# A third interleaved seven-product unit, and halves of keys and values folded by DMA, in a fused pooling-attention and SiLU kernel

## Chip, cores and metric

The kernel runs on one core of one Trainium2 chip. The metric is the device time of one execution in microseconds (us). Before the change three executions took 285.09, 285.44 and 285.60 us; the median is 285.44 us. The profile shown below is of one more execution, whose span is 284.4 us from the first to the last instruction.

## What is computed

```python
# q, k, v: (8 batches, 8 heads, 576 positions, 64), fp32
k_p = k.reshape(B, H, 72, 8, D).mean(axis=3)       # keys and values are averaged
v_p = v.reshape(B, H, 72, 8, D).mean(axis=3)       # over groups of 8 positions
attn = softmax(q @ k_p.T / sqrt(D))                # 576 x 72 for each head
x = (attn @ v_p)                                   # to (4608 tokens, 512)
h = x @ w_in                                       # 512 -> 2048
g = h * (1.0 / (1.0 + np.exp(-h)))                 # SiLU
out = g @ w_out                                    # 2048 -> 512, fp32
```

## The kernel before

The 4608 tokens are taken in nine tiles of 512 (`t` = 0 to 8). Each tile has an up-projection (`up`) with SiLU into `h_T` and then a down-projection (`down_quarters`). The attention of the batch `a = t + 1` is done in the gaps of the tile's instruction stream: a list of small functions ("fillers"), each with the number of the matmul step behind which it stands. So a filler's position fixes its place in the order of every engine's instructions; the engines themselves run each its own stream and wait for each other through semaphores.

The loads of one batch. A row of keys is 8 positions x 64 values in fp32. The first four positions are loaded plainly, and the other four are added onto them by a second load that accumulates. VectorE then adds the remaining four positions in two steps (4 to 2, and 2 to 1). All these loads are issued by GpSimd:

```python
def load_one(b, name):                       # first half: plain
    raw = raw_tile(f"{name}_raw", H)         # 72 x 8 x 256 fp32, one buffer for k, one for v
    nc.gpsimd.dma_start(out=raw, in_=source(b, name)[:, :, :PH])

def load_rest(b, name):                      # second half: added to the first by the DMA
    nc.gpsimd.dma_start(
        out=batches[b][f"{name}_raw"], in_=source(b, name)[:, :, PH:], accum_op=ALU.add)

def add_halves(raw):                         # 4 positions to 2, on VectorE (L183)
    nc.vector.tensor_add(
        out=raw[:, :, : 2 * D], in0=raw[:, :, : 2 * D], in1=raw[:, :, 2 * D :])

def add_rest(dst, raw):                      # 2 positions to 1, on VectorE (L188)
    nc.vector.tensor_add(out=dst, in0=raw[:, :, :D]..., in1=raw[:, :, D : 2 * D]...)

def pool_k(b, stage):
    if stage == 0: add_halves(raw); return
    for i in range(2): add_rest(kp[...], raw[...])

def pool_v(b):
    add_halves(st["v_raw"])
    add_rest(st["vp"]..., st["v_raw"])
```

The up-projection has 16 groups of 128 hidden columns. A plain group is four matmuls of 512 tokens, each over 128 of the 512 inputs. Four groups together can be done as one unit of the Strassen-Winograd kind: the block of 512 hidden columns by 512 tokens is split in quarters, and seven products of quarter size take the place of eight. Two units (groups 4 to 7 and 8 to 11) are done so in each tile from tile 1 on; the other eight groups are plain. A unit needs sums of quarters of the weights (made once), sums of quarters of x (`x_sum`, five per tile), and sums between its products:

```python
def stage(y, n):                                     # y: the unit, n: the step
    if n == "2":
        product(y, 2, "P", True);  nc.scalar.copy(r_sb, ps["P"])                # L499
    elif n == "5":
        product(y, 5, "Q", True);  tt(out=rr_sb, in0=ps["Q"], in1=r_sb, add)    # L502
    elif n == "1":
        product(y, 1, "R", True);  tt(out=t_sb, in0=ps["R"], in1=rr_sb, subtract)  # L505
    elif n == "4":
        product(y, 4, "P", False); hidden(y, 1, 0, ps["P"])     # SiLU on ScalarE, L490
    elif n == "3":
        product(y, 3, "Q", False); hidden(y, 0, 1, ps["Q"])
    elif n == "7":
        product(y, 7, "P", False); tt(out=c_sb[0], in0=ps["P"], in1=t_sb, add)  # L514
    elif n == "6":
        product(y, 6, "Q", False); tt(out=c_sb[1], in0=ps["Q"], in1=t_sb, add)  # L517
    elif n == "h": hidden(y, 0, 0, c_sb[0])
    else:          hidden(y, 1, 1, c_sb[1])                     # "s"
```

`product` issues four matmuls of 256 tokens (L482). P and Q stand in banks of the tag `at` (five banks, shared with the attention), R in one of the tag `mm` (three banks, shared with the plain groups, L541). `r_sb`, `rr_sb` and `t_sb` are one buffer each. The order of a tile from tile 2 on, and the fillers of loads and sums:

```python
items = (G(12, 13) + [(0, "251")] + G(14) + [(0, "43")] + G(15) + [(0, "76")]
    + [(1, "2")] + [(0, "hs")] + [(1, "51")] + G(0) + [(1, "43")] + G(1)
    + [(1, "7h6")] + G(2) + [(1, "s")] + G(3))
for n in U_X:                    # five sums of x at the head of the tile, L449
    f_up.append((0, lambda n=n: unit_x_sum(t, n)))
...
f_up.append((22, lambda: k_transpose(a)))
f_down.append((10, lambda: pool_v(a)))
...
for stage in range(2):           # the next batch's keys
    f_down.append((73 + 8 * stage, lambda stage=stage: pool_k(a + 1, stage)))
f_up.append((0, lambda: load_one(a + 1, "k")))
f_up.append((48 if a + 1 == B - 1 else 1, lambda: load_q(a + 1)))
f_up.append((2, lambda: load_rest(a + 1, "k")))
f_down.append((11, lambda: load_one(a + 1, "v")))
f_down.append((12, lambda: load_rest(a + 1, "v")))
```

The batches 3 to 7 are loaded in this way, in the tiles 1 to 5. Batches 0 to 2 are loaded and summed in another layout, which the change leaves alone.

Of the kernel before, what the change touches and what calls it, by code (L numbers as in the profile page):

```python
# [27 lines left out]
FP32 = mybir.dt.float32  # L28
FP32R = mybir.dt.float32r
BF16 = mybir.dt.bfloat16  # L30
# [6 lines left out]
def kernel(  # L37
# [73 lines left out]
    t_sb = singles.tile([128, 2, CQ], FP32, name="t_sb")  # L111
    xT = singles.tile([128, KF, NX], BF16, name="xT")

    w_sum1 = [singles.tile([128, 5, 2, 256], BF16, name=f"w_sum1{n}") for n in range(2)]
    x_sum = singles.tile([128, 5, 2, NQ], BF16, name="x_sum")
    c_sb = [singles.tile([128, 2, NQ], FP32, name=f"c_sb{n}") for n in range(2)]

# [61 lines left out]
            accum_op=ALU.add,  # L179
        )  # L180

    def add_halves(raw):
        nc.vector.tensor_add(  # L183
            out=raw[:, :, : 2 * D], in0=raw[:, :, : 2 * D], in1=raw[:, :, 2 * D :]
        )

    def add_rest(dst, raw):
# [3 lines left out]
            in1=raw[:, :, D : 2 * D].rearrange("k h (c d) -> k h c d", c=2),  # L191
        )

    def pool_k(b, stage):
        st = batches[b]
        raw = st["k_raw"]
        if stage == 0:
            add_halves(raw)
            return
        for i in range(2):  # L200
            add_rest(
                kp[:SP, i].rearrange("k c s d -> k s c d"), raw[:, 4 * i : 4 * (i + 1)]
            )

    def pool_v(b):
        st = batches[b]
        st["vp"] = mid.tile([SP, H, D], BF16, tag="vp", name="vp")
        add_halves(st["v_raw"])
        add_rest(st["vp"].rearrange("k h (c d) -> k h c d", c=2), st["v_raw"])

    def k_transpose(b, parts=(0, 1)):
# [207 lines left out]

    UNITS = ((4, 6), (8, 10))
    UW = [
        {
            (i, j): w_in_sb[:, 2 * j : 2 * j + 2, 128 * u : 128 * (u + 2)]
# [14 lines left out]
    def unit_weight_sum(y, n):  # L440
        a, b = U_W[n]
        nc.vector.tensor_tensor(
            out=w_sum1[y][:, U_WI[n]], in0=UW[y][a], in1=UW[y][b],
            op=ALU.subtract if n in (6, 7) else ALU.add,
        )

# [6 lines left out]

    def unit_weights(y, n):
        if n in U_WI:
            return w_sum1[y][:, U_WI[n]]
        return UW[y][0, 0] if n == 3 else UW[y][1, 1]

    def unit_x(t, n):
# [5 lines left out]
    def up(t, fillers, items):  # L465
        step = spread(
            fillers,
            sum(
                KF if len(it) == 3 else 2 * len(it[1].strip("hs")) for it in items
            ),  # L470
        )
        ps = {}

        def product(y, n, bank, first):
            if first:
                tag = "mm" if bank == "R" else "at"
                ps[bank] = ps_tile([128, 2, NQ], FP32, tag, f"u_ps{bank}")
            w, x = unit_weights(y, n), unit_x(t, n)
            for u in range(2):
                next(step)  # L480
                for kk in range(2):
                    nc.tensor.matmul(  # L482
                        ps[bank][:, u, :], lhsT=w[:, kk, 128 * u : 128 * (u + 1)],
                        rhs=x[:, kk, :], start=first and u == 0 and kk == 0,
                        stop=kk == 1, skip_group_check=True,
                    )

        def hidden(y, i, j, src):
            g = UNITS[y][i]
            nc.scalar.activation(  # L490
                h_T[:, g : g + 2, j * NQ : (j + 1) * NQ], src, func=AF.Silu
            )

        tt = nc.vector.tensor_tensor

        def stage(y, n):
            if n == "2":
                product(y, 2, "P", True)
                nc.scalar.copy(r_sb, ps["P"])  # L499
            elif n == "5":  # L500
                product(y, 5, "Q", True)
                tt(out=rr_sb, in0=ps["Q"], in1=r_sb, op=ALU.add)  # L502
            elif n == "1":
                product(y, 1, "R", True)
                tt(out=t_sb, in0=ps["R"], in1=rr_sb, op=ALU.subtract)  # L505
            elif n == "4":
                product(y, 4, "P", False)
                hidden(y, 1, 0, ps["P"])
            elif n == "3":
                product(y, 3, "Q", False)  # L510
                hidden(y, 0, 1, ps["Q"])
            elif n == "7":
                product(y, 7, "P", False)
                tt(out=c_sb[0], in0=ps["P"], in1=t_sb, op=ALU.add)  # L514
            elif n == "6":
                product(y, 6, "Q", False)
                tt(out=c_sb[1], in0=ps["Q"], in1=t_sb, op=ALU.add)  # L517
            elif n == "h":
                hidden(y, 0, 0, c_sb[0])
            else:  # L520
                hidden(y, 1, 1, c_sb[1])

        for it in items:
            if len(it) == 3:
                plain(t, step, *it)
            else:
                for n in it[1]:
                    stage(it[0], n)
        for _ in step:
            pass  # L530
# [248 lines left out]
    def load_half_2(name, half):  # L779
        for i0, i1 in ((0, SA), (SA, SLOTS), (SLOTS, SLOTS + 1)):  # L780
            load_slots(nc.gpsimd, 2, name, i0, i1, half)

    visits = [third(n) for n in range(3)]
    for t in range(NT):
        a = t + 1
        f_up, f_down = [], []
        if t == 0:
            GA = 11
            items = [(g, 0, HS) for g in range(GA)]
            items += [(g, HS, NTT - HS) for g in range(GA)]  # L790
            items += [(g, 0, NTT) for g in range(GA, KG)]
            f_up += [(1, lambda: denominators(0, part(0, 1), on_dve=True))]
            f_up += [(5, lambda: denominators(0, part(1, 1), on_dve=True))]
            f_up += [(13, lambda: numerators(0, part(0, 1)))]
            f_up += [(17, lambda: numerators(0, part(1, 1)))]
        else:
            G = lambda *gs: [(g, 0, NTT) for g in gs]
            if t == 1:
                items = (
                    G(12, 13, 14, 15) + [(0, "251")] + G(8) + [(0, "43")] + G(9)  # L800
                    + [(0, "7h6")] + G(10) + [(0, "s")] + G(11, 0, 1, 2, 3)
                )
            else:
                items = (
                    G(12, 13) + [(0, "251")] + G(14) + [(0, "43")] + G(15) + [(0, "76")]
                    + [(1, "2")] + [(0, "hs")] + [(1, "51")] + G(0) + [(1, "43")] + G(1)
                    + [(1, "7h6")] + G(2) + [(1, "s")] + G(3)
                )
            for n in U_X:
                f_up.append((0, lambda n=n: unit_x_sum(t, n)))  # L810
            for n in (2, 5):
                f_up.append((36 if t > 1 else 45, lambda n=n: hidden_sum(n, 4, 8)))
            f_up.append((56, lambda: hidden_sum(6, 4, 8)))
            for n, k0 in ((2, 0), (5, 0), (1, 4), (1, 0)):
                f_up.append((64, lambda n=n, k0=k0: hidden_sum(n, k0, k0 + 4)))
            f_down.append((33, lambda: hidden_sum(7, 0, 8)))
            f_down.append((71, lambda: hidden_sum(6, 0, 4)))
# [7 lines left out]
                if t == t0:  # L825
                    f_to.append((at + i, lambda n=n, i=i: weight_sum(n, i)))
        if a < B:
            q_at = [15, 16, 17, 8] if t > 1 else [24, 25, 26, 2] if t else [82, 84, 86, 88]
            if t == 0:
                for j in range(2):  # L830
                    f_up.append((44 + 8 * j, lambda j=j: slot_sums("k", j)))
# [5 lines left out]
            elif t == 1:  # L837
                for j in range(2):
                    f_up.append((0, lambda j=j: slot_sums("k", j, halves=True)))
                    f_up.append((22, lambda j=j: select_k(2, j)))  # L840
                    f_up.append((23, lambda j=j: copy_k(2, j)))
                    f_down.append((8, lambda j=j: slot_sums("v", j, halves=True)))
                    f_down.append((40, lambda j=j: select_v(2, j, "at")))
                    f_down.append((41, lambda j=j: copy_v(2, j)))
            else:
                f_up.append((22, lambda: k_transpose(a)))
                f_down.append((10, lambda: pool_v(a)))
            for n in range(4):
                f_to = f_down if t and n == 3 else f_up
                f_to.append((q_at[n], lambda n=n: q_transpose(a, n % 2, n // 2)))  # L850
            if t == 0:
                f_down.append((0, lambda: load_half_2("k", 0)))
# [5 lines left out]
                    for n in U_W:  # L858
                        f_down.append((6, lambda y=y, n=n: unit_weight_sum(y, n)))
            elif a + 1 < B:  # L860
                for stage in range(2):
                    f_down.append((73 + 8 * stage, lambda stage=stage: pool_k(a + 1, stage)))
                f_up.append((0, lambda: load_one(a + 1, "k")))
                f_up.append((48 if a + 1 == B - 1 else 1, lambda: load_q(a + 1)))
                f_up.append((2, lambda: load_rest(a + 1, "k")))
                f_down.append((11, lambda: load_one(a + 1, "v")))
                f_down.append((12, lambda: load_rest(a + 1, "v")))
            f_down.append((0, attn_tables))

            if t:  # L870
                sc_at, den_at, nu_at = (1, 31, 75), (31, 56, 97), (56, 97, 101)
            else:
                sc_at, den_at, nu_at = (1, 16, 30), (16, 30, 44), (44, 55, 56)
            for n, sg in enumerate(visits):
# [3 lines left out]
            for n, sg in enumerate(visits):  # L878
                if n < 2 or not 0 < t < B - 2:
                    f_down.append((nu_at[n], lambda sg=sg: numerators(a, sg)))  # L880
                if n == 0 and 1 < t < B - 1:
                    f_down.append((nu_at[n], lambda: numerators(a - 1, visits[2])))
        moe_tables()
        up(t, f_up, items)
        if t == 0:
# [31 lines left out]
```

The softmax here doesn't subtract the row's maximum and nothing guards it: scores larger than these inputs give would overflow.

## Time and profile before

| what | value |
|---|---|
| time, median of 3 | 285.44 us |
| span of the profiled execution | 284.4 us |
| mean granted TensorE clock | 0.999 |
| busy TensorE / VectorE / ScalarE / GpSimd | 276.5 / 225.5 / 183.6 / 61.1 us |
| middle tiles (t = 2 to 5), length | 29.10, 29.09, 29.26, 29.10 us |
| last two tiles | 25.29, 25.55 us |

In the views, L12 is line 12 of the kernel. PE is TensorE's matmuls, PEld its weight loads (beside the matmuls), DVE is VectorE, ACT ScalarE, POOL GpSimd, SP the engine that issues the stores. A group's row gives its line, engine and operation, what it writes and reads with shapes, its count, then busy time and the mean ns of one, then the idle time of the engine just before and what ended it. The slices split the span in 40 equal parts; each digit is the busy share in tenths. "To landing" is the time from a DMA's issue until its data has arrived. A tile's length is taken here from the first plain matmul of its up-projection to the next tile's.

### The profile page before, as it was taken

The page shows a single profiled execution, that of the slowest core. Times are in us where ns is not written, and L with a number is a line of the kernel's source. Part 1 is how long each engine was busy: PE and PEld are TensorE (multiplying, and loading weights), DVE is VectorE, ACT ScalarE, POOL GpSimd, SP SyncE. Part 2 cuts the span into 40 slices and gives each one's busy share as a digit, 9 for nine tenths or more (in the row PEclk, how much of TensorE's full clock was granted, in tenths as well). Part 3 has the DMA queues.
Part 4 walks back from the last instruction along what each step waited for, and adds up shares of the span by engine and source line. Part 5 has one row for each costly group of instructions (what it writes and reads, how often), then busy time and mean ns, then how long its engine had stood idle before and what let it go on. Part 6 is the DMA issues. An engine that isn't in the chain of part 4 may idle for free.

```text
span 284.4 us, 6909 instructions
## 1 busy us (share of the span) xinstructions
PE 276.5 (97%) x2793; PEld 194.4 (68%) x2793; DVE 225.5 (79%) x404; ACT 183.6 (65%) x359; POOL 61.1 (21%) x78
## 2 busy tenths in 40 slices
PE   7879999999999999999999999999999999999995
PEld 2337544466777677767888876677667767787684
DVE  3888836989978798879896998799888786836773
ACT  1677676468667876688568857785779467326700
POOL 8664215252140214021402130441100000000000
PEclk9999999999999999999999999999999999999999
DMA  7999998997849843995498539597740041005003
GB/s 193 280 243 242 208 298 176 233 151 150 153 61 217 159 108 52 187 207 97 84 183 186 95 85 172 139 142 112 120 114 0 2 101 49 2 16 133 1 17 134
DMA packets 31376, 37.70 MB, mean 133 GB/s; under 512 B 10352, under 2 KB 22256, under 8 KB 31344
## 3 DMA queue, kind: packets, MB, share of 16 engines
q0 software_dynamic: 23840, 26.77, 53.2%
q1 hardware_dynamic: 6928, 9.58, 12.3%
q10 hardware_dynamic: 576, 0.92, 1.2%
q8 instruction: 22, 0.36, 0.6%
q14 instruction: 10, 0.08, 0.1%
HBM read 36.70 MB, written 9.44 MB: 162 GB/s over the span
## 4 chain that ended last, share of the span: by engine, by line
PE 80%; DMA 15%; DVE 2%; POOL 1%; issue 1%; POOLq 0%
PE hp_ps L541 21%; PE o_psP L649 15%; PE o_psQ L649 15%; PE u_psP L482 7%; PE u_psQ L482 7%; PE o_psR L649 5%; DMA w_out_sb<-in_moe_w_out_dram 5%; DMA q_bf<-in_q_dram 4%; DMA raw<-in_k_dram 3%; DMA raw<-in_v_dram 3%; PE sc_ps L345 3%; PE u_psR L482 2%; PE nu_ps L389 2%; PE den_ps L363 2%; DVE w_sum L627 1%
## 5 line engine op out<-in xcount | busy, mean ns | idle before, releaser
L541 PE MATMUL hp_ps<-xT,w_in_sb 128*128 128x512 bf16 (+3 forms) x412 | 82.6, 340 | 0.5 <-ACT h_T L547 0.4
L649 PEld LDWEIGHTS <-h_sum 128*128 128x128 bf16 x640 | 60.6, 98 | 11.9 <-issue 1.3
L547 ACT ACTIVATE h_T<-hp_ps 128x512 bf16<-128x512 f32 (+2 forms) x95 | 51.4, 546 | 25.4 <-PE hp_ps L541 24.2
L541 PEld LDWEIGHTS <-w_in_sb 128*128 128x128 bf16 x412 | 39.3, 98 | 25.0 <-issue 1.4
L609 DVE TENSOR_TENSOR h_sum<-h_T 128x1024 bf16<-128x1024 bf16 (+1 forms) x72 | 50.9, 744 | 6.9 <-ACT h_T L547 6.9
L353 ACT ACTIVATE es<-sc_ps 72x384 bf16<-72x384 f32 (+1 forms) x100 | 39.0, 469 | 10.7 <-PE sc_ps L345 10.6
L482 PEld LDWEIGHTS <-w_sum 128*128 128x128 bf16 x300 | 29.3, 98 | 7.7
L649 PEld LDWEIGHTS <-h_T 128*128 128x128 bf16 x256 | 24.0, 98 | 4.5 <-issue 0.9
L398 DVE TENSOR_TENSOR xT<-nu_ps,rec 128x384 bf16<-128x384 f32 (+1 forms) x50 | 23.9, 532 | 0.2
L372 ACT ACTIVATE lnd<-den_ps 128x384 f32<-128x384 f32 (+1 forms) x23 | 11.1, 484 | 19.3 <-PE den_ps L363 19.3
L153 DVE STREAM_TRANSPOSE qT<-q_bf 128x576 bf16<-128x576 bf16 x32 | 23.0, 755 | 0.2 <-DMA q_bf<-in_q_dram 0.2
L490 ACT ACTIVATE h_T<-c_sb 128x512 bf16<-128x512 f32 x30 | 18.1, 625 | 5.8 <-DVE c_sb L514 5.8
L268 DVE TENSOR_TENSOR raw<-raw 128x384 f32<-128x384 f32 (+3 forms) x20 | 12.3, 617 | 8.5 <-DMA raw<-in_v_dram 5.0
L177 POOL DMA_DIRECT2D raw<-in_k_dram x5 | 7.1, 1429 | 50.6 <-DMA raw<-in_k_dram 50.6
L649 PE MATMUL o_psP<-w_out_sb,h_sum 128*128 128x256 bf16 x128 | 17.6, 273 | 0.0
L553 POOL DMA_DIRECT2D out_dram<-o_sb x1 | 0.6, 617 | 78.4 <-issue 78.4
L514 DVE TENSOR_TENSOR c_sb<-u_psP,t_sb 128x512 f32<-128x512 f32 x15 | 10.3, 689 | 8.2 <-PE u_psP L482 3.6
L649 PE MATMUL o_psQ<-w_sum,h_sum 128*128 128x256 bf16 x128 | 16.7, 273 | 0.0
L649 PE MATMUL o_psQ<-w_out_sb,h_sum 128*128 128x256 bf16 x128 | 16.6, 273 | 0.0
L649 PE MATMUL o_psQ<-w_sum,h_T 128*128 128x256 bf16 x128 | 16.5, 273 | 0.0
L649 PE MATMUL o_psP<-w_sum,h_T 128*128 128x256 bf16 x128 | 16.5, 273 | 0.0
L649 PE MATMUL o_psR<-w_sum,h_sum 128*128 128x256 bf16 x128 | 15.7, 273 | 0.0
(80 smaller groups left out, 438.8 us busy)
## 6 DMA issues: line engine op xcount, KB each, us to landing
out_dram<-o_sb SPq DMA_DIRECT2D x128, 64.0 KB, 4.2
raw<-in_k_dram POOLq DMA_DIRECT2D x10, 576.0 KB, 9.8
raw<-in_v_dram POOLq DMA_DIRECT2D x10, 576.0 KB, 8.0
q_bf<-in_q_dram POOLq DMA_DIRECT2D x6, 576.0 KB, 12.7
w_in_sb<-in_moe_w_in_dram POOLq DMA_DIRECT2D x8, 256.0 KB, 8.3
w_out_sb<-in_moe_w_out_dram POOLq DMA_DIRECT2D x4, 512.0 KB, 13.8
raw<-in_v_dram POOLq DMA_DIRECT2D x2, 768.0 KB, 11.7
raw<-in_k_dram POOLq DMA_DIRECT2D x1, 768.0 KB, 9.9
```

The costliest lines, as they stand in the source:

```text
L153: nc.vector.transpose(out=st["qT"][:, a, f * QF : (f + 1) * QF].rearrange("r i c p -> r (i c p)"), in_=st["q_bf"][:, a, f * n : (f + 1) * n],)
L268: nc.vector.tensor_add(out=raw[..., :w], in0=raw[..., :w], in1=raw[..., w : 2 * w])
L353: nc.scalar.activation(es[:, s, :], sc[s], func=AF.Exp, scale=score_scale)
L372: nc.scalar.activation(lnd, den_ps[:, :w], func=AF.Ln)
L398: nc.vector.tensor_mul(out=xT[:, 2 * g0 + c : 2 * (g0 + ng - 1) + c + 1 : 2, cols], in0=nu[c][:, :w].rearrange("r (g n) -> r g n", g=ng), ...
L482: nc.tensor.matmul(ps[bank][:, u, :], lhsT=w[:, kk, 128 * u : 128 * (u + 1)], rhs=x[:, kk, :], start=first and u == 0 and kk == 0, stop=kk ...
L490: nc.scalar.activation(h_T[:, g : g + 2, j * NQ : (j + 1) * NQ], src, func=AF.Silu)
L514: tt(out=c_sb[0], in0=ps["P"], in1=t_sb, op=ALU.add)
L541: nc.tensor.matmul(hp_ps[:, r0:r1], lhsT=w_in_sb[:, kk, g * 128 : (g + 1) * 128], rhs=xT[:, kk, x0 : x0 + r1 - r0], start=(kk == 0), stop= ...
L547: nc.scalar.activation(h_T[:, g, n0 : n0 + n], hp_ps[:, :n], func=AF.Silu)
L609: nc.vector.tensor_tensor(out=h_sum[n][:, ks, :], in0=quarter(*a, ks), in1=quarter(*b, ks), op=op)
L649: nc.tensor.matmul(ps[b][:, c, :], lhsT=left(n, kt, c), rhs=W_OUT[n][:, kt, :], start=b not in begun, stop=kt == k1 - 1, skip_group_check= ...
```

## The change

The change has three parts. From tile 2 on, groups 12 to 15 become a third seven-product unit, so that three units and four plain groups are left, and the three units' steps are interleaved by a written order. This is to take matmul columns away from TensorE. Second, the first of VectorE's two additions for keys and values is done by a DMA that reads one half of the raw tile in SBUF and accumulates it onto the other (`fold`); this is to make room on VectorE for the third unit's sums. Third, the five sums of x for a tile are taken at the end of the tile before, so that the first unit can start a tile.

```diff
-    def add_halves(raw):
-        nc.vector.tensor_add(
-            out=raw[:, :, : 2 * D], in0=raw[:, :, : 2 * D], in1=raw[:, :, 2 * D :]
+    def fold(b, name):
+        raw = batches[b][f"{name}_raw"]
+        nc.gpsimd.dma_start(
+            out=raw[:, :, : 2 * D], in_=raw[:, :, 2 * D :], accum_op=ALU.add
         )
 ... (pool_k and pool_v lose their add_halves)
-    UNITS = ((4, 6), (8, 10))
+    UNITS = ((4, 6), (8, 10), (12, 14))
 ... (banks P, Q and R are kept per unit: ps[y, bank])
+    THREE = (
+        "A2 A5 B2 A1 B5 A4 A3 C2 B4 A7 A6 Ah B1 B3 As C5 B7 C4 B6 C1 Bh C3 C7 Bs g0 C6"
+        " Ch g1 Cs g2 g3",
 ... (another order for tile 7 and another for tile 8)
             else:
-                items = (
-                    G(12, 13) + [(0, "251")] + G(14) + [(0, "43")] + G(15) + [(0, "76")]
 ...
+                items = []
+                for it in THREE[max(t - B + 2, 0)].split():
+                    items += [(("BCA".index(it[0])), it[1])] if it[0] in "ABC" else G(int(it[1]))
-            for n in U_X:
-                f_up.append((0, lambda n=n: unit_x_sum(t, n)))
+            if t < 2:
+                for n in U_X:
+                    f_up.append((0, lambda n=n: unit_x_sum(t, n)))
 ... (positions of h_sum, q_transpose, scores and denominators)
-                f_up.append((22, lambda: k_transpose(a)))
-                f_down.append((10, lambda: pool_v(a)))
+                f_up.append((0, lambda: k_transpose(a)))
+                f_down.append((12, lambda: pool_v(a)))
 ...
-                for stage in range(2):
-                    f_down.append((73 + 8 * stage, lambda stage=stage: pool_k(a + 1, stage)))
+                f_down.append((81, lambda: pool_k(a + 1)))
                 f_up.append((0, lambda: load_one(a + 1, "k")))
                 f_up.append((48 if a + 1 == B - 1 else 1, lambda: load_q(a + 1)))
                 f_up.append((2, lambda: load_rest(a + 1, "k")))
-                f_down.append((11, lambda: load_one(a + 1, "v")))
-                f_down.append((12, lambda: load_rest(a + 1, "v")))
+                f_up.append((3, lambda: fold(a + 1, "k")))
+                f_down.append((13, lambda: load_one(a + 1, "v")))
+                f_down.append((14, lambda: load_rest(a + 1, "v")))
+                f_down.append((15, lambda: fold(a + 1, "v")))
 ...
+        if 0 < t < B:
+            for n in U_X:
+                f_down.append((44 if t == B - 1 else 98, lambda n=n: unit_x_sum(t + 1, n)))
+        if t == 1:
 ... (the third unit's weight sums: two tiles in the freed buffers of batch 2's rows)
+            for n in U_W:
+                f_down.append((73, lambda n=n: unit_weight_sum(2, n)))
```

## The prediction

> **What bounds the kernel now.** I read the busy shares and the slices of the page first.
>
> ```profile
> PE 276.5 (97%) x2793; PEld 194.4 (68%) x2793; DVE 225.5 (79%) x404; ACT 183.6 (65%) x359; POOL 61.1 (21%) x78
> PE   7879999999999999999999999999999999999995
> PEclk9999999999999999999999999999999999999999
> ```
>
> TensorE works at 90% or more in every slice but three at the start and the last, at full clock. Then the busy time in the stretch of one middle tile (t = 3; columns: stretch, length, then busy time and instructions per engine, clock, DMA share, GB/s).
>
> ```profile
> 112.96:142.05 29.09, 29.09 (x314) 21.47 (x313) 25.34 (x42) 21.48 (x42) 5.31 (x6) 1.00 0.74 144
> ```
>
> The tile has no TensorE gap: 29.09 us of 29.09. VectorE is at 25.34 (87%), ScalarE at 21.48 (74%). So a middle tile gets shorter only if TensorE gets less work, and longer if any other chain needs more than 29.09 us per tile. The chain that ended last, in order of time, gives the price of the two kinds of work in the up-projection (start, length, group):
>
> ```profile
> 86.90 0.86 PE hp_ps L541 x4
> ...
> 90.07 0.44 PE u_psQ L482 x4
> ```
>
> One plain group is four matmuls of 512 columns, 0.865 us (two groups read 1.73 elsewhere in this chain); one product of a seven-product unit is four of 256 columns, 0.437 us (eight of these read 0.87 in the down-projection).
>
> Last the chain that I came to distrust: GpSimd, which issues the loads of q, k and v. It is 21% busy, but it stands still on waits (who waited for whom: total, times, longest):
>
> ```profile
> POOL raw L177 <- DMA raw<-in_k_dram: 50.6, 5, 11.6
> POOL raw L177 <- DMA raw<-in_v_dram: 16.0, 3, 5.6
> ```
>
> L177 is the adding load of the second half of a row group. It is not issued until the first half has landed, and everything behind it in GpSimd's stream waits too. GpSimd in order of time, one period of it (start, length, issue, idle before and who ended it):
>
> ```profile
> 123.47 1.43 POOL L177 DMA_DIRECT2D raw<-in_k_dram  x1 [10.44 <-DMA raw<-in_k_dram]
> 132.23 0.83 POOL L173 DMA_DIRECT2D raw<-in_v_dram  x1 [7.32 <-DVE vp L188]
> 138.12 1.40 POOL L177 DMA_DIRECT2D raw<-in_v_dram  x1 [5.06 <-DMA raw<-in_v_dram]
> 139.54 0.83 POOL L173 DMA_DIRECT2D raw<-in_k_dram  x1
> 140.36 0.75 POOL L145 DMA_DIRECT2D q_bf<-in_q_dram  x1
> 152.18 1.43 POOL L177 DMA_DIRECT2D raw<-in_k_dram  x1 [11.06 <-DMA raw<-in_k_dram]
> ```
>
> Call the four loads k1, k2, v1, v2. From k2 to k2 is 28.71 us, the tile's period; only 7.32 us of it is slack (v1 waits for VectorE to free its buffer). The landing times of k2 at 123.47 and of v1 at 132.23, from the list of the raw tile:
>
> ```profile
> DMA to landing us min/median/max: 8.1/8.1/8.1
> ...
> DMA to landing us min/median/max: 5.6/5.6/5.6
> ```
>
> Over the five rounds k2 took 7.7, 8.3, 8.1, 8.7, 9.6 and v1 6.2, 5.8, 5.6, 5.8, 6.8. v2, with k1 issued right behind it, took 9.1 to 10.4, and k1 behind v2 11.4 to 12.5.
>
> [...] the 10.44 us before k2 is idle time of GpSimd. [...] So the new folds, which read what k2 and v2 write, must wait for their landing; the existing k2 does so for k1. [...]
>
> **Part 1, the third unit (tiles 2 to 8).** It removes four plain groups per tile, 4 x 0.865 = 3.46 us, and adds seven products, 7 x 0.437 = 3.06 us: TensorE gains 0.40 us per tile, 2.8 us over seven tiles. It costs, per tile, one copy and four activations on ScalarE where four activations were (one more, 0.58 us), and four VectorE operations:
>
> ```profile
> L499 ACT COPY r_sb<-u_psP 128x512 f32<-128x512 f32 x15 | 8.7, 583 | 5.4 <-PE u_psP L482 5.4
> L502 DVE TENSOR_TENSOR rr_sb<-u_psQ,r_sb 128x512 f32<-128x512 f32 x15 | 10.4, 692 | 6.0 <-ACT r_sb L499 6.0
> ...
> L183 DVE TENSOR_TENSOR raw<-raw 72x1024 f32<-72x1024 f32 x10 | 12.0, 1197 | 0.0
> ```
>
> Four such operations are 0.69 x 4 = 2.76 us of VectorE. The up-projection then holds three units with 3 x 3.0 us of ScalarE and four groups of 0.6: 11.4 us of about 12.6, in order, and r_sb, rr_sb and t_sb are one buffer each for three interleaved units. I allow 0.1 to 0.2 us of stalls per tile, 1 us in all.
>
> **Part 2, the folds.** They remove two L183 operations per tile, 2 x 1.2 = 2.4 us of VectorE: with part 1 VectorE goes from 25.3 to about 25.7 of 28.7 us, so it does not become the bound. In exchange GpSimd's stream becomes k1, q, k2, kf, v1, v2, vf, where kf waits for k2 and vf for v2. kf alone would be free: k2 lands at 131.6 and v1 was issued only at 132.23. vf is not: k1 of the next batch, issued 1.4 us after v2 today, stands behind the landing of v2. The new round, with a fold's issue put at 1.4 us as an accumulating load's is:
> - k1 to k2: alone k1 should land like v1, 5.8; with vf ahead of it in the same DMA engines, and q behind it, I put 8.3 with the step.
> - k2 to kf: 8.2 + 0.3 = 8.5. kf to v1: 1.4.
> - v1 to v2: 5.8 alone, with kf beside it about 8.0.
> - v2 to vf: 8.5 (8.2 as k2, for k1 no longer competes). vf to k1: 1.4.
> Sum 36 us; without any contention 5.8 + 8.5 + 1.4 + 6.1 + 8.5 + 1.4 = about 32. Either is longer than the tile's 28.7.
>
> How long a fold takes to land I estimate from k2 (590 KB in 8.2 us, 1.4 of it issue) and v1: a fold moves half the bytes in as many pieces of half the length, so between 5.4 us (by bytes) and 8.2 (by pieces); I use 6.
>
> Now the deadline, the key's add on VectorE at step 81 of the down-projection. In tile 1 k2 goes out at 67.88 and lands at 75.6; kf lands about 82, and the add stood at 80.3. One round of 36 later kf of the next batch lands at 118, and tile 2 wants it at 110; then 154 against 138.7, 190 against 167.4, and about 225 against 196 in tile 5, the last that folds a key. Waiting in VectorE's stream holds up the evictions, the products into xT and the sums of x behind it, and with them the next tile's first products; I allow 1.5 us of slack once. So the tiles end 225 - 196 - 1.5 = 27 us late at a round of 36, about 21 at 34.5, and 11 at 32. The last q load stands behind kf too and may cost 1 to 2 us in tile 6.
>
> **Part 3, the sums of x a tile ahead.** Five operations of 0.42 us (x_sum, L449) move from the head of a tile to the end of the tile before. They take no VectorE time away; they let unit A start without plain groups ahead. Worth nothing alone. The five weight sums of the third unit (2.1 us, once, in tile 1) lie in VectorE's slack.
>
> Sum: 285.4 - 2.8 + 1 + 21 (round of 34.5, between the two) = 304.6; I lean a little lower, 303.
>
> **Rivals.** (a) The round fits: folds land in some 4 us, k1 and v1 in 5.6, k2 and v2 in 7.7, each fold's issue 0.9. Then the round is 29 us, the deadlines hold, and only part 1 is left: 285.4 - 2.8 + 0.5 = about 283. For it: every one of these landings is the fastest the trace shows for its kind, and the schedule was clearly laid out round by round. Against: they would all have to be the fastest at once, with one more transfer in the same engines, whose share is already 0.74. (b) ScalarE and the single r_sb, rr_sb, t_sb stall the three units, 0.5 to 1 us per tile: 286 to 290. For it: 11.4 of 12.6 us and the 1.28 us table load at the tile's head; against: today's waits of that kind (rr_sb for r_sb) are 6.0 us over 15 units, all on VectorE and none on TensorE. (c) VectorE as the bound: 25.7 of 28.7, only bunched; worth 1 us at most.
>
> **Range and chances.** The chain of loads follows from the issue order and from measured landings; only its length is an estimate, 29 at the very best and 37 at the worst, which is 283 to 314. I give the long round three chances in four. Slower by over 2% begins at 291.1, which is a delay of 8.6 us or a round of 31.4. Faster by over 2% would need 279.7, more than all that part 1 can give.
>
> **What would show it.** Right: GpSimd waits of some 8 us ahead of both folds; the period of k2 to k2 above 31 us in tiles 2 to 5; VectorE idle before the key's add, ended by a DMA; tiles 2 to 5 longer than 30 us with TensorE gaps, and tiles 7 and 8 shorter than before by some 0.4 us. Wrong: a period near 28.7 and no such idle time, so a time of 282 to 284; or gaps inside the up-projection instead, ended by ScalarE or VectorE, which is rival (b).

## Result, and the profile after

The changed kernel takes 338.0 us (median of 6, 337.91 to 339.25) against 285.21 us before (median of 6): a ratio of 1.186, 95% interval 1.184 to 1.188. The direction was predicted, the size was not: 303 was forecast, 314 the upper end, and the loss is 52.8 us. Here and in the experiments below, an execution more than 1.5% above the fastest of its kernel counts as slow and is left out of medians and ratios: one of four with the folds' traffic and no wait (300.32 us), and five of six with both folds and first halves by SyncE, where the full range stands instead.

Busy shares, TensorE's slices and its granted clock, from the page of the changed kernel (span 336.0 us):

```profile
PE 285.6 (85%) x2845; PEld 204.8 (61%) x2861; DVE 232.8 (69%) x427; ACT 189.1 (56%) x366; POOL 74.6 (22%) x88
PE   8899999999999409997299964999259979989995
PEclk9999999999999956999679995999859999999999
```

TensorE's row now has four holes in its middle (their lowest slices are 0, 2, 4 and 2), and at each the granted clock falls (lowest slices 5, 6, 5 and 5). Before there was none. TensorE in order of time shows the holes; the bracket is the idle time ahead of the instruction and who ended it:

```profile
125.17 0.64 PE L216 MATMUL kT_ps<-shifts,kp 128*128 128x72 bf16 x4 [11.96 <-DVE kp L193]
...
165.70 0.64 PE L216 MATMUL kT_ps<-shifts,kp 128*128 128x72 bf16 x4 [8.05 <-DVE kp L193]
...
206.24 0.63 PE L216 MATMUL kT_ps<-shifts,kp 128*128 128x72 bf16 x4 [7.81 <-DVE kp L193]
...
247.41 0.70 PE L216 MATMUL kT_ps<-shifts,kp 128*128 128x72 bf16 x4 [10.11 <-DVE kp L193]
```

Each time TensorE stands at the transpose of the next batch's keys and waits for VectorE's add of those keys (kp). In the list of who waited for whom, that add in turn waits for the fold:

```profile
PE kT_ps L216 <- DVE kp L193: 37.9, 4, 12.0
...
DVE kp L193 <- DMA raw<-raw: 39.9, 4, 15.2
```

And here is one round of GpSimd, from k2 to k2 (start, length, issue, idle before and who ended it). L177 is a plain half, L181 an adding half, L188 a fold, L149 q:

```profile
65.83 1.43 POOL L181 DMA_DIRECT2D raw<-in_k_dram  x1 [7.01 <-DMA raw<-in_k_dram]
73.55 1.39 POOL L188 DMA_DIRECT2D raw<-raw  x1 [6.28 <-DMA raw<-in_k_dram]
74.38 1.41 POOL L177 DMA_DIRECT2D raw<-in_v_dram  x1
85.89 1.40 POOL L181 DMA_DIRECT2D raw<-in_v_dram  x1 [10.10 <-DMA raw<-in_v_dram]
96.17 1.38 POOL L188 DMA_DIRECT2D raw<-raw  x1 [8.87 <-DMA raw<-in_v_dram]
96.98 1.42 POOL L177 DMA_DIRECT2D raw<-in_k_dram  x1
97.81 1.34 POOL L149 DMA_DIRECT2D q_bf<-in_q_dram  x1
109.36 1.43 POOL L181 DMA_DIRECT2D raw<-in_k_dram  x1 [10.21 <-issue]
```

The order is k1, q, k2, kf, v1, v2, vf, as the diff has it, and four waits for a DMA stand in it, one after the other, where two stood before beside one for VectorE (7.32 us, the slack that the prediction counted). For the last of the four the view names no releaser; the k1 issued at 96.98 landed 11.2 us later, at 108.2. The rounds last 43.5, 40.4, 39.9 and 40.5 us (k2 at 65.83, 109.36, 149.73, 189.66 and 230.17): 41.1 on average, where a tile's own work is 28.7. Before, k2 to k2 was 28.5 on average (67.88 to 181.70 in four rounds).

The whole loss can be read off one instruction, the last batch's key add, before and after:

```profile
196.85 0.75 DVE L188 TENSOR_TENSOR kp<-raw 72x256 bf16<-72x256 f32 x2
246.93 0.82 DVE L193 TENSOR_TENSOR kp<-raw 72x256 bf16<-72x256 f32 x2 [13.33 <-DMA q_bf<-in_q_dram]
```

It starts 50.1 us later. The view puts this wait down to a piece of q, but the fold issued at 238.16 took 8.7 us and so landed at the same moment, 246.9; this add reads what it wrote. From there to the end it was 87.55 us and is 89.1: another 1.5. Together this is the 51.6 us between the two profiled spans.

### The profile page after: what moved, and what is told of

Read it like the earlier page. It is cut to its first block, busy times and chain, and to the rows that moved or that the text cites. A ratio compares the mean times of both kernels' runs of the same rounds, so it can differ in the third digit from the quotient of the medians.

```text
span 336.0 us, 7099 instructions
## 1 busy us (share of the span) xinstructions
PE 285.6 (85%) x2845; PEld 204.8 (61%) x2861; DVE 232.8 (69%) x427; ACT 189.1 (56%) x366; POOL 74.6 (22%) x88
## 5 line engine op out<-in xcount | busy, mean ns | idle before, releaser
L482 PEld LDWEIGHTS <-w_sum 128*128 128x128 bf16 x440 | 45.7, 105 | 13.1 <-DVE xT L398 2.1
L541 PE MATMUL hp_ps<-xT,w_in_sb 128*128 128x512 bf16 (+3 forms) x273 | 51.7, 332 | 1.1 <-ACT h_T L547 0.4
L353 ACT ACTIVATE es<-sc_ps 72x384 bf16<-72x384 f32 (+1 forms) x100 | 39.1, 470 | 10.5 <-PE sc_ps L345 10.4
L193 DVE TENSOR_TENSOR kp<-raw 72x256 bf16<-72x256 f32 x10 | 3.8, 418 | 53.2 <-DMA raw<-raw 39.9
L547 ACT ACTIVATE h_T<-hp_ps 128x512 bf16<-128x512 f32 (+2 forms) x67 | 34.7, 526 | 10.0 <-PE hp_ps L541 8.4
L541 PEld LDWEIGHTS <-w_in_sb 128*128 128x128 bf16 x284 | 27.1, 98 | 18.3 <-issue 1.4
L216 PE MATMUL kT_ps<-shifts,kp 128*128 128x72 bf16 x20 | 2.7, 237 | 38.1 <-DVE kp L193 37.9
L490 ACT ACTIVATE h_T<-c_sb 128x512 bf16<-128x512 f32 x44 | 27.5, 630 | 5.3 <-DVE c_sb L514 4.1
L188 POOL DMA_DIRECT2D raw<-raw x10 | 13.9, 1385 | 74.3 <-DMA raw<-in_k_dram 33.3
L499 ACT COPY r_sb<-u_psP 128x512 f32<-128x512 f32 x22 | 12.9, 587 | 23.4 <-DVE rr_sb L502 16.5
L216 PEld LDWEIGHTS <-kp 128*128 128x128 bf16 x20 | 1.3, 108 | 39.9 <-DVE kp L193 39.9
L372 ACT ACTIVATE lnd<-den_ps 128x384 f32<-128x384 f32 (+1 forms) x23 | 11.2, 485 | 20.4 <-PE den_ps L363 20.4
L482 PEld LDWEIGHTS <-w_in_sb 128*128 128x128 bf16 x176 | 18.0, 102 | 5.0 <-issue 1.5
L505 DVE TENSOR_TENSOR t_sb<-u_psR,rr_sb 128x512 f32<-128x512 f32 x22 | 15.0, 683 | 5.5 <-PE u_psR L482 4.1
## 6 DMA issues: line engine op xcount, KB each, us to landing
raw<-in_v_dram POOLq DMA_DIRECT2D x2, 768.0 KB, 11.2
```

Of the source, the lines that this page charges most:

```text
L188: nc.gpsimd.dma_start(out=raw[:, :, : 2 * D], in_=raw[:, :, 2 * D :], accum_op=ALU.add)
L353: nc.scalar.activation(es[:, s, :], sc[s], func=AF.Exp, scale=score_scale)
L482: nc.tensor.matmul(ps[y, bank][:, u, :], lhsT=w[:, kk, 128 * u : 128 * (u + 1)], rhs=x[:, kk, :], start=first and u == 0 and kk == 0, stop ...
L490: nc.scalar.activation(h_T[:, g : g + 2, j * NQ : (j + 1) * NQ], src, func=AF.Silu)
L499: nc.scalar.copy(r_sb, ps[y, "P"])
L505: tt(out=t_sb, in0=ps[y, "R"], in1=rr_sb, op=ALU.subtract)
```

## Experiments

"Theory W" is that the folds' waits in GpSimd's stream make its round longer than a tile; "T" that the folds' traffic slows the other loads; "U" that the interleaved units stall; "C" that the lowered clock costs time. The "round" is always the mean of four, from the first adding key load in tile 1 to the last in tile 5.

| run | median us | ratio to before, 95% interval | round us |
|---|---|---|---|
| changed kernel | 338.0 | 1.186 (1.184 to 1.188) | 41.1 |
| no folds | 284.47 | 0.996 (0.994 to 0.997) | 28.2 |
| folds alone, on the kernel before | 336.29 | 1.179 (1.176 to 1.181) | 40.2 |
| traffic, no wait | 291.82 | 1.022 (1.018 to 1.026) | 30.9 |
| wait, no traffic | 298.84 | 1.047 (1.044 to 1.051) | 32.8 |
| keys' fold only | 304.36 | 1.065 (1.060 to 1.070) | 32.6 |
| values' fold only | 300.31 | 1.051 (1.048 to 1.055) | 33.3 |
| keys' fold only, reader later | 311.84 | 1.091 (1.089 to 1.094) | 33.9 |
| gaps filled with matmuls | 338.29 | 1.187 (1.184 to 1.190) | 40.9 |
| first halves by SyncE, both folds | 292.88 to 303.79 | none given | 30.7 |
| first halves by SyncE, keys' fold | 292.69 | 1.024 (1.023 to 1.026) | 29.3 |
| first halves by SyncE, no fold | 284.22 | 0.995 (0.994 to 0.996) | not bound by it |
| no folds, sums of x at the head | 286.89 | 1.006 (1.005 to 1.007) | 28.4 |

Each ratio is to executions of the kernel before in the same set, so it can differ from a ratio to 285.21.

### The folds taken back, and the folds alone

```diff
 # no folds: the changed kernel with
+                for stage in range(2):
+                    f_down.append((73 + 8 * stage, lambda stage=stage: pool_k(a + 1, stage)))
-                f_down.append((81, lambda: pool_k(a + 1)))
-                f_up.append((3, lambda: fold(a + 1, "k")))
-                f_down.append((15, lambda: fold(a + 1, "v")))
 # ... and add_halves on VectorE again
```

Expected:

> The changed kernel with both folds taken back (VectorE adds the halves again, at steps 73 and 12); the third unit and the early sums of x stay. Theory W (the folds' waits in GpSimd's stream): no long gaps on TensorE, the round of k2 to k2 back near 28.7 us, the time 285.2 - 2.8 + 0 to 1 = 282.4 to 283.5 us. Theory U (the interleaved units are what stalls): still above 320 us. VectorE then holds 25.3 + 2.8 = 28.1 us of work per tile of 28.7; if that binds, 284 to 288 us.

Expected of the folds alone:

> The kernel before with the folds alone (keys' fold behind k2, values' fold behind v2, the two VectorE additions gone; two units, sums of x at the tile's head). Theory W: a round of about 40 us as in the changed kernel, and four gaps ended by the folds: 330 to 342 us. Theory U: 285 us, within 1%.

Without folds the time is 284.47 us; with nothing but the folds it is 336.29. So the folds are the whole loss, and U falls. TensorE of the folds-alone kernel, who waited for whom:

```profile
PE hp_ps L543 <- DVE xT L400: 22.2, 3, 10.1
PE hp_ps L543 <- DVE o_sb L682: 16.1, 2, 8.2
```

The waits are as long as in the changed kernel (38.3 us against 37.9), only at another place: there the tile starts with plain groups and meets the late VectorE at their banks and their x. The transpose of the keys at the head of the tile, also new, is therefore only where the wait shows.

The kernel without folds also shows the third unit by itself. TensorE in order of time, the third bank's products of the down-projection, in two tiles in a row:

```profile
100.41 0.38 PE L658 MATMUL o_psR<-w_sum,h_sum 128*128 128x256 bf16 x2
...
129.11 0.38 PE L658 MATMUL o_psR<-w_sum,h_sum 128*128 128x256 bf16 x2
```

The same place stood at 101.73 and 130.83 before: the tile is 28.70 us long instead of 29.10, the 0.40 that the prediction worked out. Its page has VectorE at 86% of the span, and in the middle tile's stretch at 97%:

```profile
111.00:140.00 29.00, 29.00 (x329) 22.89 (x327) 27.99 (x48) 22.45 (x44) 6.34 (x8) 1.00 0.72 140
```

### The wait and the traffic apart

```diff
 # traffic, no wait: on the kernel without folds
+    spare = singles.tile([96, 6, 2 * D], FP32); nc.vector.memset(spare, 0.0)
+    def fold(b, name):        # in the folds' places: 576 pieces of 512 bytes, no load waited for
+        nc.gpsimd.dma_start(out=spare, in_=spare, accum_op=ALU.add)
 # wait, no traffic: on the kernel without folds
+    def fold(b, name):        # in the folds' places: one piece of 512 bytes, waits for k2 (v2)
+        nc.gpsimd.dma_start(out=spare[name], in_=batches[b][f"{name}_raw"][:1, 0, 2 * D :],
+                            accum_op=ALU.add)
```

Expected of the traffic:

> The first kernel of this set plus two DMAs per batch in the places of the folds, with a fold's 576 pieces of 512 bytes, accumulating in SBUF, but on a spare tile, so that they wait for no load. The traffic is there, the wait is not. Theory W: within 2 us of the kernel without folds, 283 to 286 us. Theory T (the fold's traffic slows the loads beside it): loads of 9 to 12 us as in the changed kernel, a round above 33 us, the time above 300 us.

Expected of the wait:

> The first kernel of this set plus, in the place of each fold, a DMA of one piece of 512 bytes that reads what k2 (v2) wrote, so that it waits for its landing, and that nothing waits for. The wait is there, the traffic is not. Theory W: round = k1 6.5 + k2 8.3 + small 1 + v1 6 + v2 8.3 + small 1 = about 31 to 33 us, 3 us per tile over the tile's length, the deadline being now k2's landing at step 73: 290 to 300 us. Theory T: 283 to 285 us.

The wait alone costs 14.4 us over the kernel without folds, as W expected. GpSimd in order of time, wait without traffic (L184 adding half, L190 the small DMA, L180 plain half):

```profile
131.87 1.42 POOL L184 DMA_DIRECT2D raw<-in_k_dram  x1 [5.03 <-DMA raw<-in_k_dram]
139.66 0.83 POOL L190 DMA_DIRECT2D sparek<-raw  x1 [6.37 <-DMA raw<-in_k_dram]
140.24 1.14 POOL L180 DMA_DIRECT2D raw<-in_v_dram  x1
147.06 1.39 POOL L184 DMA_DIRECT2D raw<-in_v_dram  x1 [5.68 <-DMA raw<-in_v_dram]
156.83 0.80 POOL L190 DMA_DIRECT2D sparev<-raw  x1 [8.37 <-DMA raw<-in_v_dram]
157.41 1.11 POOL L180 DMA_DIRECT2D raw<-in_k_dram  x1
```

k1 to k2 takes 7.2 us here in the mean of the four rounds, v1 to v2 6.9. In the changed kernel, with a fold just ahead of each, the same two steps take 11.6 and 10.1. The traffic alone costs 7.4 us (its executions scatter from 289.98 to 293.36, and one took 300.32), so that it is slower is clear and whether by over 2% is not: neither W's 2 us nor T's 15 and more. Its GpSimd shows why it costs anything (L191 the spare DMA):

```profile
130.66 1.46 POOL L191 DMA_DIRECT2D sparek<-sparek  x1
132.28 0.86 POOL L180 DMA_DIRECT2D raw<-in_v_dram  x1
143.72 1.39 POOL L184 DMA_DIRECT2D raw<-in_v_dram  x1 [10.58 <-DMA raw<-in_v_dram]
```

v1 lands 11.2 us after its issue at 132.28, and 5.6 to 6.8 in the kernel before. So both theories hold a part, and the parts do more than add up: 14.4 + 7.4 is 21.8 us, and the changed kernel lost 53.5 against the one without folds. By the rounds: 28.2 without folds, 32.8 with the waits, 30.9 with the traffic, 41.1 with both. With the traffic alone, slack in the round hides part of each slowed load: the steps k1 to k2 and v1 to v2 are together 7.1 us longer in a round than without folds, but the time from k2 to v1, where v1 stood waiting for VectorE, shrinks from 7.6 to 3.4 us, so the round grows by 2.8 only. With the waits, no such slack is left and every slowed load is waited for in full: the 32.8 us of the waits, plus the 4.4 and 3.2 us by which the two steps are longer behind a fold, are 40.4 of the 41.1 measured.

### One fold at a time, and its reader later

```diff
 # keys' fold only: the values' halves are added by VectorE again; values' fold only: the reverse
 # reader later: keys' fold only, and
-                f_down.append((81, lambda: pool_k(a + 1)))
+                f_up.append((12, lambda: pool_k(a)))            # in the next tile
-                f_up.append((0, lambda: k_transpose(a)))
+                f_up.append((26, lambda: k_transpose(a)))
 # k1, q, k2, kf of the next batch at steps 12 to 15 instead of 0 to 3
```

Expected of the keys' fold:

> The changed kernel with the values' fold taken back (VectorE adds the values' halves), the keys' fold kept. Theory W: the wait of kf for k2 costs nothing in GpSimd's stream, for v1 waited there anyway (6.4 to 7.7 us without folds); k1 follows v2 again at once. What is left is the deadline: k2 lands about 132 in tile 3, kf 7 us later, 139.5, where the key's add stood at 137.5, and k1 of the next batch waits for that add; a round of 29 to 30.5 us, the time 286 to 295 us. Theory T (mainly the folds' traffic): half of the 53 us, 310 us.

Expected of the values' fold:

> The changed kernel with the keys' fold taken back, the values' fold kept. Theory W: vf puts the landing of v2 ahead of the next k1. Round = k1 to k2 11.5 (vf beside it) + k2 to v1 1.4 + v1 to v2 8 + v2 to vf 9.3 + 0.8 = about 31 to 32 us, deadline k2's landing at step 73: 292 to 302 us, more than the keys' fold alone. Theory T: the same as the keys' fold alone, some 310 us.

Expected of the later reader:

> The keys' fold alone, and its reader moved: the key's add and its transpose stand in the next tile's up-projection (steps 12 and 26), and k1, q, k2 and kf of the next batch behind them. Theory W: kf has then some 6 us more to land, its wait is hidden, no gap: 282.5 to 284.5 us, at or a little below the kernel without folds, as VectorE loses 1.2 us of its 28.0 per tile. If the traffic alone holds things up, 287 to 292 us.

The values' fold alone lies in W's range (300.31), but not above the keys' fold, as W had it: that one took 304.36, more than W's 286 to 295, though still below T's 310. GpSimd, keys' fold only:

```profile
99.43 1.43 POOL L181 DMA_DIRECT2D raw<-in_k_dram  x1 [9.92 <-DMA raw<-in_k_dram]
109.05 1.40 POOL L188 DMA_DIRECT2D raw<-raw  x1 [8.20 <-issue]
109.89 1.42 POOL L177 DMA_DIRECT2D raw<-in_v_dram  x1
119.69 1.37 POOL L181 DMA_DIRECT2D raw<-in_v_dram  x1 [8.38 <-DMA raw<-in_v_dram]
120.51 1.40 POOL L177 DMA_DIRECT2D raw<-in_k_dram  x1
...
132.29 1.42 POOL L181 DMA_DIRECT2D raw<-in_k_dram  x1 [9.63 <-DMA raw<-in_k_dram]
```

k2 to v1 is 10.5 us, of which 9.6 pass before kf goes out, and v1 to v2 is 9.8. Without folds the same steps were 7.9 (123.98 to 131.84) and 5.9 (to 137.79). So kf is not free even where v1 had been waiting anyway: v1 to v2 then takes 3.9 us longer with kf just ahead of it, the largest part of the round's growth.

The later reader was the worst of the three, 311.84 where 282.5 to 284.5 was expected. The expectation took the reader's deadline for the bound. But the cycle k1, k2, kf, v1, v2, k1 closes in GpSimd's own stream, whatever the reader does; its round is 33.9 us. Then the edit made something new late: the last batch's q, issued behind kf. VectorE, in order of time:

```profile
225.67 0.78 DVE L157 STREAM_TRANSPOSE qT<-q_bf 128x576 bf16<-128x576 bf16 x1 [13.62 <-DMA q_bf<-in_q_dram]
```

### The lowered clock

```diff
     def k_transpose(b, parts=(0, 1)):
 ...
+        if b > 3:
+            fill_ps = ps_tile([128, 512], FP32, "mm", "fill_ps")
+            for _ in range({4: 52, 5: 34, 6: 34, 7: 42}[b]):
+                nc.tensor.matmul(fill_ps, lhsT=warm[:, :128], rhs=warm, start=True, stop=True)
```

Expected:

> The changed kernel with extra matmuls of zeros ahead of the key's transpose in tiles 3 to 6 (52, 34, 34 and 42 of 512 columns, some 7 to 11 us each), so that TensorE works through most of each gap and its clock need not fall; they add no result. Theory C (the half clock after each gap, some 5 us long, is part of the loss): the mean clock from 0.939 to above 0.985 and the time 8 to 12 us down, 326 to 330 us. Theory W (the round of loads sets the time, TensorE's slow start is absorbed by the next wait): the clock up, and the time within 3 us of 338.

The stretches of the first gap and of the 6 us behind it, changed kernel and then filled (length, then TensorE, weight loads, VectorE, ScalarE, GpSimd, clock, DMA share, GB/s):

```profile
113.00:125.00 12.00, 0.21 (x2) 0.00 (x0) 0.31 (x1) 0.50 (x1) 2.24 (x2) 0.71 0.67 101
125.00:131.00 6.00, 5.41 (x26) 3.27 (x27) 5.97 (x14) 1.57 (x3) 1.38 (x1) 0.50 0.43 98
```

```profile
113.00:125.00 12.00, 12.00 (x64) 5.79 (x62) 1.68 (x4) 1.01 (x1) 2.24 (x2) 1.00 0.58 93
125.00:131.00 6.00, 5.06 (x47) 4.07 (x44) 5.83 (x13) 2.68 (x6) 1.38 (x1) 1.00 0.66 115
```

The clock is back at 1.00 in both stretches, and on the mean at 0.990 from 0.939; the time is 338.29 us, unchanged. C falls. The reading that fits is that TensorE at a granted clock of 0.50 for 6 us behind a gap only makes the next wait shorter, as long as the loads set the pace.

### The waits taken out of one stream

```diff
-        nc.gpsimd.dma_start(out=raw, in_=source(b, name)[:, :, :PH])     # k1, v1
+        nc.sync.dma_start(out=raw, in_=source(b, name)[:, :, :PH])
 ... (k1 at the head of the tile only in tile 1)
+                if a + 2 < B:
+                    f_down.append((82, lambda: load_one(a + 2, "k")))    # ahead of the stores
```

Expected, both folds:

> The changed kernel with both folds, but k1 and v1 issued by SyncE (k1 of the next batch right behind the key's add, ahead of the tile's stores), so that GpSimd's stream holds only q, k2, kf, v2, vf and its waits overlap with those loads. The folds' traffic stays whole. Theory W+T (the round is the sum of the landings that GpSimd's stream waits for in turn): round = q and k2 9.5 + kf 0.8 + v2 10 + vf 0.8 + wait for v1 some 4 = 25 to 28 us, under the tile's 28.7, so no long gap: 282 to 286 us. If the traffic by itself is what sets the time, still above 300 us.

Expected, keys' fold:

> The same with the values' fold taken back (VectorE adds the values' halves). Theory W+T: GpSimd's round shorter by vf, less traffic ahead of k1, VectorE at 26.8 us per tile: 282 to 284.5 us, no gap.

Expected, no fold:

> The same with no fold at all: the third unit and early sums of x, k1 and v1 on SyncE. VectorE is as full as in the kernel without folds, 28.0 us per tile. If VectorE's 28.0 is what keeps that kernel at 284.5 instead of 282.6, this stays within 0.5 us of 284.5 and the two with folds are faster; if not, the three are alike.

With GpSimd rid of k1 and v1, both folds cost 7 to 18 us over the kernel before instead of 53, and the keys' fold alone 7 instead of 19. The ordering was most of the loss, but not all: 282 to 286 was expected with both folds, 282 to 284.5 with one. The edit changes the issuing engine and the place of k1 along with the waits; without folds the same edit leaves the time as it was (284.22 us against 284.47). What is left shows in the version with the keys' fold, whose four executions lie close together (291.86 to 293.3). SyncE's own waits, and VectorE's:

```profile
SPq L177 <- DMA raw<-raw: 34.4, 4, 11.5
```

```profile
DVE kp L198 <- DMA raw<-raw: 13.3, 5, 4.4
```

k1 of the next batch waits until the fold of this one has landed, for the keys have one buffer, and VectorE's add of the keys waits for that fold in all five tiles. So the keys alone go round k1, k2, kf, add, in 30.1 us (adds at 83.75 and 204.35, four rounds apart) where the SyncE version without folds has 28.6 (80.80 and 195.22). The last add stands 9.1 us later than there, and the span is 8.6 us longer. That this loop is the remaining bound is read from the trace and not tried: a second buffer was not built. Without folds, the SyncE version is the lowest of all here, 0.5% below the kernel before; the no-folds kernel is within its interval. Whether VectorE's 28.0 us per tile holds these two back stays open, for the versions with a fold are slower for another reason.

### The sums of x back at the head

```diff
-            if t < 2:
-                for n in U_X:
-                    f_up.append((0, lambda n=n: unit_x_sum(t, n)))
+            for n in U_X:
+                f_up.append((0, lambda n=n: unit_x_sum(t, n)))
 # on the kernel without folds; the sums a tile ahead are gone
```

Expected:

> The changed kernel without folds and without the early sums: the five sums of x stand at the head of their own tile again, so the third unit is all that is left of the change. If part 3 is worth nothing by itself, this is within 0.5 us of the kernel without folds (284.5 us). If unit A, which now starts the tile with no plain group ahead, waits for its sums, each of tiles 2 to 8 starts 1 to 2 us late: 290 to 297 us.

286.89 us, between the two expectations: the early sums are worth 2.4 us. The third unit without them is 0.6% slower than the kernel before. The same wait of 0.31 us stands in each of tiles 2 to 6:

```profile
115.18 0.60 PE L491 MATMUL u_psQ<-x_sum,w_in_sb 128*128 128x256 bf16 x4 [0.31 <-DVE rr_sb L511]
```

Two tiles in a row are 29.16 us apart here (129.24 less 100.08, the same products as above), 0.46 more than with early sums; 0.31 of it is this wait. TensorE waits for rr_sb, which VectorE takes up only at 114.44, straight behind the five sums of x (from 112.77). The remaining 0.15 was not traced.

## Why the prediction was right and wrong

**What bounds the kernel.** Right: a middle tile has no TensorE gap, so it could only get longer by another chain, and GpSimd's stream was that chain.

**Part 1.** Right for a middle tile, together with the early sums: 0.40 us were worked out and 0.40 measured. In all 1.8 us were expected after stalls, and the medians differ by 0.9 (285.39 and 284.47). The profiled spans do differ by 1.8 (284.4 and 282.6), but the one of before belongs to an execution of 286.33 us, above the median of 285.44. One stall is seen: in tile 7 TensorE waits 1.1 us for h_sum in the kernel without folds, and not at all there before.

**Part 2, the order of the waits.** Right: kf waits for k2, vf for v2, and k1 stands behind the landing of v2. The prediction's ground in the traces was k2's wait for k1 (10.44 us in the round it shows); what a fold without its wait would do to the keys was not shown. The marks named as proof came: waits of 6.3 to 8.9 us ahead of both folds, a round above 31 us, VectorE idle ahead of the key's add until a DMA ends it, TensorE gaps in those tiles, and a last tile 0.42 us shorter (24.87 us from the third products of tile 7 to those of tile 8, 25.29 before). Tile 7 was not shorter: from its up-projection to that of tile 8 it took 26.0 us (281.29 to 307.30) against 25.3, with the same wait of 1.1 us for h_sum in it.

**Part 2, the length of the round.** This is the step that failed: the time that a load takes with a fold just ahead of it. "Sum 36 us", then "a round of 34.5, between the two", "37 at the worst"; measured 41.1. Its terms, with the means of four rounds:

| step | predicted us | measured us |
|---|---|---|
| k1 to k2 | 8.3 | 11.6 |
| k2 to kf | 8.5 | 8.1 |
| kf to v1 | 1.4 | 0.8 |
| v1 to v2 | 8.0 | 10.1 |
| v2 to vf | 8.5 | 9.6 |
| vf to k1 | 1.4 | 0.8 |
| sum | 36.1 | 41.1 |

The mis-sized terms are the two loads right behind a fold, +3.3 and +2.1 us, and v2, +1.1; the issues were 0.6 us too long each. A load behind a fold was given 2.2 to 2.5 us for contention; it takes 3.2 and 4.4 (6.9 and 7.2 us without a fold ahead, 10.1 and 11.6 with one), and those 6.9 and 7.2 are already above the 5.8 put for the load alone. The fold itself was sized well: 6 us were put, and where nothing follows it (vf at 264.69) it took

```profile
DMA to landing us min/median/max: 6.3/6.3/6.3
```

while with a load right behind folds took 6.8 to 7.9, and the last batch's keys' fold, with q behind it, 8.7. (By bytes the prediction's own figures give 4.8 and not 5.4: half of the 6.8 us beyond the issue, and the issue. The 6 that it used stays near the 6.3.) q behind k1 matters less: the last k1, with no q behind it, still landed in 10.7 us, against 11.2 with q. The second fault was to pull the 36 down to 34.5 towards a sum without contention, which no run reached with both folds in GpSimd's stream. Four rounds of 41.1 - 34.5 are 26.4 us, which brings the prediction's sum of 304.6 to 331. Of the 7 us still missing, 2.7 lie in the delay of the last key's add: counted as in the prediction it comes to 27 + 4 x 5.1 = 47.4 us, and it was 50.1. The 1.5 us of slack were not there, and 82 + 4 x 36 is 226, not 225. Another 3.3 lie behind that add. The sum took off 1.8 us for the third unit, but in tiles 2 to 5 the loads set the pace and the gain cannot be had, and from the add to the end the kernel took 1.5 us more than before. There the last batch's v loads stand behind its late q: the last fold of values holds VectorE's read of v for 4.1 us and TensorE for 1.5 us in tile 6; tile 7 adds its 1.1 us. The last 1 us is that the profiled execution of before was slower than the median.

**"kf alone would be free."** Wrong: 20 us over the kernel without folds. It saw the wait hidden and not the load that the fold slows (v1 to v2 9.8 us against 5.9).

**Part 3.** The prediction gave the early sums no term of their own; beside the third unit they are worth 2.4 us. The reason was in the same paragraph: the sums let unit A start a tile without plain groups ahead. "Worth nothing alone", on the kernel with two units, was not tried.

**Rivals.** (a), the fitting round, would have needed every landing at its fastest; none of the loads behind a fold was. (b) shows once and small: the middle tiles without folds are 28.70 us, as worked out, and only in tile 7 does TensorE wait 1.1 us for h_sum, ahead of which VectorE had waited 0.6 us for ScalarE's h_T. (c) VectorE came to 97% in a middle tile without folds and still let TensorE run through (29.00 us of 29.00); its relief by one fold, 26.8 us of work per tile, bought nothing that could be seen beside the fold's cost.

## What to carry to other kernels

An issuing engine's stream is a cycle: add up its waits over one round and compare the sum with the time of a round of work, and do it again whenever a DMA that depends on another is put into it: here the waits became the pace when the round went from 28.5 to 41.1 us, past the 28.7 of the tile's own work. Size a load beside new traffic by what the trace shows for two transfers in a row, not by its landing when alone (v1 landed in 5.6 to 6.8 us before, and in 9.1 to 10.7 right behind a fold). Moving work from an engine with slack to a DMA is no gain in itself: here 2.4 us of VectorE per tile, all of it beside other work, was bought with 12.6 us of GpSimd's round (28.5 to 41.1).

## What the runs showed of the hardware

A DMA of 295 KB that accumulates within SBUF took 6.3 us with no load behind it, about as long as a plain load of 590 KB of values took in the kernel before (5.6 to 6.8), and the step of the load issued 0.8 us behind one was 3.2 and 4.4 us longer (10.1 and 11.6 us against 6.9 and 7.2). After TensorE's gap of 12 us in tile 3 the granted clock was 0.50 for the next 6 us, and this cost nothing in time here: with the gaps filled the clock was 1.00 and the time the same within 0.3 us.
